# An attention + routed experts + FFN kernel on one Trainium2 core: eight instead of twelve weight-conversion units left to the FFN, rows scaled behind another block, a PSUM bank for the small slot's transposes

## The chip, the cores and the metric

The kernel runs on one core of one Trainium2 chip. The metric is device microseconds (us) of one execution, the median of several runs; lower is better. The engines are named as the profile names them: PE (TensorE, matmuls; PEld is its loading of weights), DVE (VectorE), ACT (ScalarE), POOL (GpSimd) and SP (SyncE, which issues most of the DMAs; SPq is its queue).

## The reference

Three layers follow each other; everything is float32.

```python
# 1. attention, 4 x 12 heads, sequence 448, head size 64
scores = scale * q @ k.T - log(S);  attn = sigmoid(scores);  x = attn @ v
x = x.transpose(0, 2, 1, 3).reshape(1792, 768)
# 2. experts: each row goes to one of 8 experts
expert_idx = argmax(normalised(x) @ normalised(expert_emb).T / tau);  gate_w = its softmax probability
h = maximum(x[mask] @ w1[e], 0)            # w1[e] 768 x 1024
out[mask] = gate_w[mask] * (h @ w2[e])     # w2[e] 1024 x 768
# 3. FFN
h = x @ w_in                               # 768 x 2048
g = h - tanh(h)
return g @ w_out                           # 2048 x 768
```

## The kernel before

A float32 product is made of three matmuls on operands that are split into a rounded high part and the rest (the low part): high by high, high by low, low by high. Splitting an operand costs a cast on ACT (high) and a subtraction on DVE (low). Three stretches follow each other: attention (to about 225 us), the experts (225 to 538 us) and the FFN in two halves of the rows (half 0 to about 793 us, half 1 to 1041 us), then the last scatter of output rows.

**Experts.** The rows that were routed to an expert are gathered into groups. Two groups with rows of the first three batches, `s0` and `s1`, come first, then six slots of up to 256 rows; a further "small slot" of at most 128 rows (`few`) runs behind slot 0. A group is one pass of `group`. It has four blocks `c` of w1: `product` makes two times 18 matmuls into the PSUM tile `pth`, ACT writes the relu `hh` (L925) and DVE its low part `hl` (L926). Then come three blocks of w2, two times 24 matmuls each, into `pty`. `split` (L896 to L899) makes each product's weights ready: ACT casts the raw weights to `ring`, DVE subtracts; `ring` holds four products. So PE waits for ACT's and DVE's splits, and a w2 block also for `hl`.

The next group's rows (`prep`, called by `nxt()` between the w1 and the w2 blocks) are gathered by a DMA that POOL issues (L800), scaled by their gate on ACT (`gate_rows`, L809; in slot 1 on POOL, L818), transposed on PE into `xt` (L840), and split again (ACT L846, DVE L847) into `wi0` and `xl`. When ACT may scale them is set by `issue_after`: for the second group behind the third block's relu, otherwise by `last_few` or by the scheduler.

In the small slot the operands' parts are exchanged: `product` of `few` has the rows as the loaded operand and the weights as the moving one, so that its result has to be turned: `keep` stores it on ACT, `turn` transposes it back on PE into a tile of the `xt` buffers, and `hidden` or `out` read that. `both(c, h)` splits half h of the c-th weight block for it.

**Conversion units.** The FFN's weights come as float64 words. A unit (`conv_steps`) turns one block of 128 columns of w_in or 128 rows of w_out into high and low float32 parts: SP loads `cr` (L1164), ACT takes the absolute value of the high words (L1169), DVE runs four instructions over `ca` (L1171, L1173, L1175, L1177), ACT casts (L1180), DVE subtracts (L1182), SP stores to DRAM (`dwi`, `dwo`, L1184). There are 32 units, in the order wi0, wo0, wi1, wo1 and so on. One runs early in attention; `CPG` says how many run in each group of the experts as long as more than `NFFN` are left; the rest run in FFN half 0, up to `CPF` for each chunk. The experts have three `cr` buffers; the FFN has one, so that its units run one after the other.

**FFN.** In half 0, `act` loads the blocks `wi` and `wo` of f = 0 to 15 from DRAM (L1266, L1269), makes z = y @ w_in (36 matmuls for each f, 18 over 512 and 18 over 384 columns, L1277) and g - tanh on ACT and DVE into `gh` and `gl`; `outp` takes a chunk of two f and adds g @ w_out to the accumulators: 84 matmuls of 384 columns (L1328), seven additions on DVE (L1341). `split(1)` then makes half 1's operands. Half 1 loads the same blocks again.

The order of instructions on each engine is set when the program is built, by the library's scheduler, which works with priorities (`high_priority`) and `issue_after`; each engine then runs its list in order.

```python
                with tc.issue_after(self.xg_act.ins):
                    for _ in range(conv.pop(0)):
                        if len(self.units) > NFFN:
                            with tc.high_priority(offset=LATER):
                                self.conv_unit(*self.units.pop(0), after=self.last_w)
```

In the FFN the same call of `conv_unit` stands in the loop over chunks, behind `act`.

Of the kernel before, what the change touches and what calls it, by code (L numbers as in the profile page):

```python
# [21 lines left out]
LAG = 4  # L22
ROW = 2
ROUTE, ROUTE_E = 8, 3
NEARLY, NFFN = 1, 12
CONV = 14
CPG, CPF = (2, 3, 0, 3, 3, 3, 3, 2), 2
IDLE = 9
LATER = -600
EARLY = -100  # L30
# [2 lines left out]
P = 128  # L33
# [8 lines left out]
class Prog:  # L42
# [721 lines left out]

    def experts_early(self, cx):

        self.last_few = None
        self.pp = self.pool("plan", 1, cx)
        self.mrec = self.pool("mrec", 2, cx)
        self.mx = self.pool("mx", 1, cx)  # L770
        self.mrow = self.pool("mrow", 1, cx)
        wr = self.pool("mrawa", 1, cx)
        self.raws = [wr.tile([P, self.NJ, 256], F32, name=f"w1raw{c}") for c in range(NWE)]
# [31 lines left out]
    def gate_rows(self, s, h):  # L805

        DM, x = self.DM, s["x"]
        with self.tc.issue_after(self.last_few) if self.last_few is not None else ExitStack():
            self.xg_act = self.nc.scalar.activation(x[:, h, :DM], x[:, h, :DM], AF.Copy, scale=x[:, h, DM + 1 : DM + 2])  # L809

    def gather_rows(self, pl, slot, pool=False):
# [61 lines left out]
    def experts(self, cx):  # L873
# [14 lines left out]
        self.last_y = None  # L888
        ps = self.pool("mps", 2, cx, space=PSUM)
        hps = self.pool("mph", 2, cx, space=PSUM, side="right")  # L890

        turns = [0]

# [21 lines left out]
        def group(s, e, new, off, have, nxt, conv, mid=None, last=False, inner=None):  # L915
            hh = hp.tile([P, KF, GR], F32R, tag="hh", name="hh")
            hl = hp.tile([P, KF, GR], F32R, tag="hl", name="hl")
            for c in range(NC1):
                if c >= have:
                    self.weight(e, new, c)  # L920
                pt = hps.tile([P, 2, GR], F32, tag="h", name="pth")
                for u in range(2):
                    product(pt, self.raws[c], s["xt"], NJ, u)
                fs = slice(2 * c, 2 * c + 2)
                relus.append(nc.scalar.activation(hh[:, fs], pt, AF.Relu))  # L925
                nc.vector.scalar_tensor_tensor(hl[:, fs], pt, 0.0, f32(hh[:, fs]), ALU.max, ALU.subtract)  # L926
                if c == 0 and mid is not None:
                    mid()
            self.keep_numbers(s)
            if inner is not None:  # L930
                for c in range(NC2):
                    self.weight(e, new, NC1 + c)
            if nxt is not None:
                nxt()
            if conv:
                with tc.issue_after(self.xg_act.ins):
# [4 lines that stand above are left out]
            for c in range(NC2):  # L941
                if inner is None:
                    self.weight(e, new, NC1 + c)
                if last and c == NC2 - 1:
                    pt = self.last_y = self.lp.tile([P, 2, GR], F32, name="pty_last")
                else:
                    pt = ps.tile([P, 2, GR], F32, tag="y", name="pty")
                for u in range(2):
                    product(pt, self.raws[NC1 + c], (hh, hl), KF, u)
                if pt is not self.last_y:  # L950
                    nc.scalar.copy(self.yT[c][:, :, off], pt)
                if c == 1 and inner is not None:
                    inner()
                if last and c == NC2 - 2:
                    with tc.issue_after(self.last_mm.ins):
                        tc.mark_branch_hint_location("more", "LikelyTaken", engines=[mybir.EngineType.PE])
# [68 lines left out]
        def few(s, nxt):  # L1025
# [18 lines left out]
                return self.yT[k % 3][:, :, NT + P : NT + 2 * P]  # L1044

            def turn(k):
                pt = pst()
                for u in range(2):
                    T(nc.tensor.transpose, pt[:, u, :P], stage(k)[:, u], self.ident)
                return pt[:, :, :P]  # L1050
# [10 lines left out]
            def out(c):  # L1061
                A(nc.scalar.copy, self.yT[c][:, :, ds(oa, P)], turn(NC1 + c))
# [19 lines left out]
            for c in range(NC2):  # L1082
# [6 lines left out]
                    nxt()  # L1089
                else:  # L1090
                    out(c - 1)
                product(NC1 + c, pt, (hh, hl), 1)
                keep(NC1 + c, pt, nc.scalar.copy)
                if c == 0:
                    both(NC1 + 2, 0)
                    both(NC1 + 2, 1)
            T.last = None
            out(NC2 - 1)
            self.last_few = A.last
            turns[0] += 2 * (NC1 + NC2 - 1)  # L1100

        def run(slots, s, conv, first):
# [22 lines left out]
            pl.update(self.plan())  # L1125

        def second():
            with tc.issue_after(relus[-2].ins):
                for h in range(2):
                    self.gate_rows(self.s1, h)  # L1130
            self.columns(self.s1, pst)

        conv = list(CPG)
# [4 lines left out]
        run(list(range(NST)), s, conv, False)  # L1138
        first = lambda: nc.sync.dma_start(f32(self.wi0).rearrange("p a b -> p (a b)"), self.win_s[0].rearrange("p a b -> p (a b)"))
        first()  # L1140
        self.last_few = None
        if NG > NST:
            tot = nc.values_load(self.tot_i[0:1, 0:1], min_val=1, max_val=NG)
            with tc.If(tot > NST, label="more"):
# [319 lines left out]
```

## Time and profile before

| | |
|---|---|
| median of 3 runs | 1051.7 us (1049.59 to 1053.12) |
| profiled execution | 1050.43 us, span in the trace 1048.7 us |
| mean granted TensorE clock | 0.984 |
| PE busy | 992.3 us (95%) |
| DVE busy | 769.3 us (73%) |
| ACT busy | 587.4 us (56%) |
| POOL busy | 222.2 us (21%) |

The profiled execution took 1.7 us more than its span. PE is busy nearly all of the time, so what is to be looked for is the few places where it is not, or where its clock is lowered (a clock of 1.00 is 2.4 GHz, 0.5 is 1.2 GHz). A mean over the span doesn't show those; they are read stretch by stretch.

### The profile page before, as it was taken

What the parts mean: (1) busy time and instruction counts of PE and PEld (TensorE: products, weight loads), DVE (VectorE), ACT (ScalarE), POOL (GpSimd) and SP (SyncE); (2) the same over time, 40 slices, a digit from 0 to 9 for tenths busy, and PEclk for the clock granted to TensorE, in tenths of its full rate; (3) what the DMA queues carried; (4) which work ended last, traced back from release to release, by engine and by line L of the source; (5) the groups of instructions that cost most, each with busy time, mean ns of one, the idle gap of its engine ahead of it and who ended that gap; (6) DMA issues with size and microseconds to landing.
All of it is one profiled execution on the core that took longest, in us unless ns stands there. A gap on an engine that the chain in (4) does not pass through costs nothing.

```text
span 1048.7 us, 16583 instructions
## 1 busy us (share of the span) xinstructions
PE 992.3 (95%) x6318; PEld 921.7 (88%) x6318; DVE 769.3 (73%) x1011; ACT 587.4 (56%) x728; POOL 222.2 (21%) x315
## 2 busy tenths in 40 slices
PE   7999999999999899999999999999819999999997
PEld 5877877789999799999998999988819999999997
DVE  7687777769795699788638887788638766666773
ACT  7788888875575776666536643453217533433340
POOL 8567667554403110300000000000000300000002
PEclk9999999999999999999999999999959999999999
DMA  6433333479459859658326454434355522332312
GB/s 173 138 108 109 103 92 103 154 230 365 169 184 301 271 182 336 218 177 285 128 101 237 134 190 158 180 143 188 113 188 211 194 81 103 121 121 94 117 61 106
DMA packets 83446, 174.87 MB, mean 167 GB/s; under 512 B 7624, under 2 KB 62943, under 8 KB 83359
## 3 DMA queue, kind: packets, MB, share of 16 engines
q1 hardware_dynamic: 79438, 155.56, 43.4%
q0 software_dynamic: 3760, 17.95, 4.9%
q8 instruction: 52, 0.85, 0.3%
q14 instruction: 36, 0.29, 0.1%
q10 hardware_dynamic: 160, 0.21, 0.1%
HBM read 156.28 MB, written 36.30 MB: 184 GB/s over the span
## 4 chain that ended last, share of the span: by engine, by line
issue 57%; PE 6%; POOL 2%; DMA 1%; DVE 0%; ACT 0%; POOLq 0%; ACTq 0%; DVEq 0%
PE pth L908 3%; PE pty L908 2%; POOL out_dram L546 2%; DMA xg<-x_tok,gidx 1%; PE pty L1007 0%; ACT xg L809 0%; PE xt L840 0%; POOLq L1459 0%; DVE ring L899 0%; DVE ca L1175 0%; PE xt L1007 0%; ACT ca L1169 0%; DVE ca L1171 0%; DVE hl L926 0%; DVE xl L847 0%
## 5 line engine op out<-in xcount | busy, mean ns | idle before, releaser
L1328 PE MATMUL o<-wo,gh 128*128 128x384 f32 x896 | 239.7, 336 | 16.9 <-DMA wo<-dwo 12.2
L1277 PE MATMUL z<-yh,wi 128*128 128x512 f32 (+1 forms) x768 | 219.6, 367 | 13.8 <-DMA wi<-dwi 13.4
L1328 PEld LDWEIGHTS o<-wo,gh 128*128 128x128 f32 x896 | 163.3, 188 | 19.6 <-issue 12.5
L1277 PEld LDWEIGHTS z<-yh,wi 128*128 128x128 f32 x768 | 142.3, 189 | 30.5 <-DMA wi<-dwi 13.9
L1328 PE MATMUL o<-wo,gl 128*128 128x384 f32 x448 | 150.4, 336 | 0.0
L908 PE MATMUL pth<-wi,ring 128*128 128x256 f32 x768 | 141.7, 284 | 4.7 <-DVE hl L926 4.0
L546 POOL DMA_INDIRECT out_dram<-acc,toki x14 | 17.4, 1240 | 597.5 <-DVE acc L1341 596.3
L1277 PE MATMUL z<-yl,wi 128*128 128x384 f32 (+1 forms) x384 | 138.9, 366 | 0.0
L908 PE MATMUL pty<-hh,ring 128*128 128x256 f32 x736 | 136.2, 283 | 0.0
L908 PEld LDWEIGHTS pth<-wi,ring 128*128 128x128 f32 x768 | 119.8, 190 | 5.8 <-issue 3.7
L277 DVE TENSOR_TENSOR al<-pq,ah 128x896 fp32r<-128x896 f32 x84 | 91.2, 1087 | 42.8 <-ACT pq L276 42.4
L1341 DVE TENSOR_TENSOR acc<-o,acc 128x768 f32<-128x768 f32 x97 | 92.3, 951 | 38.1 <-PE o L1328 37.8
L908 PEld LDWEIGHTS pty<-hh,ring 128*128 128x128 f32 x736 | 115.7, 191 | 0.1
L908 PE MATMUL pth<-xl,ring 128*128 128x256 f32 x384 | 108.3, 282 | 0.0
L275 ACT ACTIVATE ah<-pq,bias_s 128x896 fp32r<-128x896 f32 x84 | 85.4, 1017 | 34.8 <-PE pq L268 34.1
L908 PE MATMUL pty<-hl,ring 128*128 128x256 f32 x368 | 103.9, 284 | 0.0
L1328 PEld LDWEIGHTS o<-wo,gl 128*128 128x128 f32 x448 | 84.4, 188 | 1.0
L276 ACT ACTIVATE pq<-pq,bias_s 128x896 f32<-128x896 f32 x84 | 83.0, 988 | 0.0
L1277 PEld LDWEIGHTS z<-yl,wi 128*128 128x128 f32 x384 | 72.4, 189 | 7.9
L899 DVE TENSOR_TENSOR ring<-w1raw,ring 128x768 fp32r<-128x768 f32 x64 | 60.5, 952 | 21.4 <-ACT ring L898 21.1
L908 PEld LDWEIGHTS pth<-xl,ring 128*128 128x128 f32 x384 | 73.2, 191 | 0.0
L1298 ACT ACTIVATE s<-t,sq_thr 128x896 f32<-128x896 f32 x32 | 33.5, 1046 | 70.2 <-DVE r L1295 70.2
(319 smaller groups left out, 1903.9 us busy)
## 6 DMA issues: line engine op xcount, KB each, us to landing
w1raw<-in_moe_w_dram SPq DMA_DIRECT2D x36, 768.0 KB
w2raw<-in_moe_w_dram SPq DMA_DIRECT2D x27, 1024.0 KB
wi<-dwi SPq DMA_DIRECT2D x32, 768.0 KB
wo<-dwo SPq DMA_DIRECT2D x32, 768.0 KB
cr<-in_moe_w_in_dram SPq DMA_DIRECT2D x16, 768.0 KB
dwi<-cr SPq DMA_DIRECT2D x16, 768.0 KB
cr<-in_moe_w_out_dram SPq DMA_DIRECT2D x16, 768.0 KB
dwo<-cr SPq DMA_DIRECT2D x16, 768.0 KB
```

What stands on the lines that cost most here:

```text
L275: nc.scalar.activation(hi, pv, AF.Sigmoid, **sc)
L276: self.last_sig = nc.scalar.activation(pv, pv, AF.Sigmoid, **sc)
L277: nc.vector.tensor_tensor(lo, pv, f32(hi), ALU.subtract)
L546: i = self.nc.gpsimd.indirect_dma_start(**kw)
L899: self.last_split = nc.vector.tensor_tensor(wl, cols, f32(wh), ALU.subtract)
L908: self.last_mm = nc.tensor.matmul(pt[:, u], a[:, kk], b[:, kk], start=(n == 0), stop=(n == 3 * K - 1))
L1277: nc.tensor.matmul(z[:, G0[g] : G0[g] + GS[g]], wi[:, a, j * P : (j + 1) * P], yhl[half][g][b][:, j], start=(left[g] == 3 * NJ), stop=(lef ...
L1298: nc.scalar.activation(s2, t, AF.Relu, bias=bias[2])
L1328: nc.tensor.matmul(o[:, w, :NW], a[:, u, i * P : (i + 1) * P], wo[:, b, w * NW : (w + 1) * NW], start=(n == 0), stop=(n == 3 * CH - 1),)
L1341: nc.vector.tensor_tensor(acc[i], ov, acc[i], ALU.add)
```

## The change

Four edits. First, the numbers of conversion units: the FFN keeps 8 instead of 12, and the experts take 23 instead of 19, with one more in the groups `s0`, slot 2, slot 3 and slot 4. Second, ACT may scale the next group's rows only behind the relu of the third of the four w1 blocks, now for every group. Third, `turn` of the small slot takes its PSUM tile from a pool of its own (`mpt`, one buffer) instead of the `xt` buffers. Fourth, in the small slot the second half of the last w2 block is split in the middle of the following block.

```diff
-NEARLY, NFFN = 1, 12
+NEARLY, NFFN = 1, 8
 CONV = 14
-CPG, CPF = (2, 3, 0, 3, 3, 3, 3, 2), 2
+CPG, CPF = (3, 3, 0, 3, 4, 4, 4, 2), 2
...
     def gate_rows(self, s, h):
 
         DM, x = self.DM, s["x"]
-        with self.tc.issue_after(self.last_few) if self.last_few is not None else ExitStack():
+        with self.tc.issue_after(self.rows_after) if self.rows_after is not None else ExitStack():
...
         hps = self.pool("mph", 2, cx, space=PSUM, side="right")
+        tps = self.pool("mpt", 1, cx, space=PSUM)
...
             if nxt is not None:
+                self.rows_after = relus[-2].ins
                 nxt()
...
             def turn(k):
-                pt = pst()
+                pt = tps.tile([P, 2, GR], F32, tag="t", name="tt")
...
                     nxt()
                 else:
                     out(c - 1)
+                if c == 1:
+                    both(NC1 + 2, 1)
                 product(NC1 + c, pt, (hh, hl), 1)
                 keep(NC1 + c, pt, nc.scalar.copy)
                 if c == 0:
                     both(NC1 + 2, 0)
-                    both(NC1 + 2, 1)
             T.last = None
             out(NC2 - 1)
-            self.last_few = A.last
...
         def second():
-            with tc.issue_after(relus[-2].ins):
-                for h in range(2):
-                    self.gate_rows(self.s1, h)
+            self.rows_after = relus[-2].ins
+            for h in range(2):
+                self.gate_rows(self.s1, h)
```

The lines of the changed kernel are numbered one or two higher than before (L908 becomes L909, L1007 L1009, L1184 L1186, L1266 L1268). A number behind a name (`dwi_116`) tells one buffer from another: of `dwi` and `dwo`, block f of w_in is `dwi_` and 88 + 2f, block f of w_out `dwo_` and 89 + 2f, so that `dwi_118` and `dwo_119` are those of f = 15.

Three places show how instructions move. The first is SP's queue at the end of FFN half 0. `cr` loads and `dwi` or `dwo` stores are conversion units; `wi` and `wo` are the FFN's loads. Before:

```order
L1164 DMA cr<-in_moe_w_in_dram 128x6x256
L1184 DMA dwi_116<-cr 128x1536
L1266 DMA wi_124<-dwi_116 128x1536
L1164 DMA cr<-in_moe_w_out_dram 128x1536
L1266 DMA wi_124<-dwi_88 128x1536
L1184 DMA dwo_117<-cr 128x1536
L1269 DMA wo<-dwo_117 128x1536
L1164 DMA cr<-in_moe_w_in_dram 128x6x256
L1184 DMA dwi_118<-cr 128x1536
L1266 DMA wi_9954<-dwi_118 128x1536
```

And now:

```order
L1166 DMA cr<-in_moe_w_in_dram 128x6x256
L1268 DMA wi_10002<-dwi_114 128x1536
L1268 DMA wi_124<-dwi_116 128x1536
L1186 DMA dwi_118<-cr 128x1536
L1166 DMA cr<-in_moe_w_out_dram 128x1536
L1271 DMA wo<-dwo_113 128x1536
L1271 DMA wo<-dwo_115 128x1536
L1268 DMA wi_10002<-dwi_118 128x1536
L1186 DMA dwo_119<-cr 128x1536
L1268 DMA wi_124<-dwi_88 128x1536
```

Before, each load of a `wi` or `wo` stood right behind the store that it reads; now the last stores stand ahead of loads of earlier blocks, `dwo_119` ahead of half 1's first load (`dwi_88`).

The second place is ACT's list from the end of the small slot into the w1 blocks of slot 1. `ring` casts are splits of slot 1's weights, `xg` is the next slot's rows, `ca<-cr` a conversion unit. Before:

```order
L1007 COPY yT_last<-xt 128x2x128
L809 ACTIVATE xg<-xg 128x768 x4
L1169 ACTIVATE ca<-cr 128x768
L898 CAST ring<-w1raw_142 128x768
L1169 ACTIVATE ca<-cr 128x768
L925 ACTIVATE hh<-pth 128x512
L898 CAST ring<-w1raw_2714 128x768 x2
L925 ACTIVATE hh<-pth 128x512
```

And now:

```order
L1009 COPY yT_last<-tt 128x2x128
L899 CAST ring<-w1raw_142 128x768
L926 ACTIVATE hh<-pth 128x512
L899 CAST ring<-w1raw_2714 128x768 x2
L926 ACTIVATE hh<-pth 128x512
L899 CAST ring<-w2raw_2715 128x1024 x2
L926 ACTIVATE hh<-pth 128x512
L809 ACTIVATE xg<-xg 128x768 x2
L1171 ACTIVATE ca<-cr 128x768 x2
L899 CAST ring<-w2raw_2716 128x1024 x2
L926 ACTIVATE hh<-pth 128x512
```

The rows' scaling and the conversion units went from ahead of the slot's second w1 block to behind its third relu (the fourth relu and two splits are now behind them).

The third place is the end of DVE's list for the experts, in the last slot (the names are those of `split`, `hl` and the conversion units; the `TENSOR_LOAD` is the experts' last row). Before:

```order
L926 SCALAR_TENSOR_TENSOR hl<-pth,hh 128x512
L899 TENSOR_TENSOR ring<-w1raw_2714,ring 128x768 x2
L926 SCALAR_TENSOR_TENSOR hl<-pth,hh 128x512
L899 TENSOR_TENSOR ring<-w2raw_2715,ring 128x1024 x2
L926 SCALAR_TENSOR_TENSOR hl<-pth,hh 128x512
L899 TENSOR_TENSOR ring<-w2raw_2716,ring 128x1024 x2
L926 SCALAR_TENSOR_TENSOR hl<-pth,hh 128x512
L899 TENSOR_TENSOR ring<-w2raw_2717,ring 128x1024 x2
L1143 TENSOR_LOAD tot_i
```

And now:

```order
L900 TENSOR_TENSOR ring<-w2raw_2716,ring 128x1024
L927 SCALAR_TENSOR_TENSOR hl<-pth,hh 128x512
L1179 SCALAR_TENSOR_TENSOR ca<-cr,ca 128x768
L1173 TENSOR_SCALAR ca<-ca 128x768
L1175 TENSOR_SCALAR ca<-ca 128x768
L900 TENSOR_TENSOR ring<-w2raw_2717,ring 128x1024
L1177 SCALAR_TENSOR_TENSOR ca<-cr,ca 128x768
L1184 TENSOR_TENSOR cr<-ca,cr 128x768
L1179 SCALAR_TENSOR_TENSOR ca<-cr,ca 128x768
L900 TENSOR_TENSOR ring<-w2raw_2717,ring 128x1024
L1184 TENSOR_TENSOR cr<-ca,cr 128x768
L1145 TENSOR_LOAD tot_i
```

Before, no conversion instruction stood in this stretch; now seven stand among the last splits. From the last-but-one slot's fourth `hl` to the end of the experts it is 30 instructions of conversion units on DVE, where it was 10.

## Rows read from the trace of the kernel before

**Rows 1.** The page's busy line: busy us (share of the span) xinstructions

```profile
PE 992.3 (95%) x6318; PEld 921.7 (88%) x6318; DVE 769.3 (73%) x1011; ACT 587.4 (56%) x728; POOL 222.2 (21%) x315
```

**Rows 2.** Waits of PE: who waits <- what ended it: us, times, longest

```profile
PE z L1277 <- DMA wi<-dwi: 13.4, 1, 13.4
PE o L1328 <- DMA wo<-dwo: 12.2, 1, 12.2
PE o L1328 <- DVE acc L1341: 4.7, 5, 1.9
PE pth L908 <- DVE hl L926: 4.0, 3, 3.0
PE xt L1007 <- DVE row L852: 1.2, 1, 1.2
```

**Rows 3.** PE's timeline, 748 to 790 us: start, duration, instructions [idle before, its releaser]

```profile
748.81 0.62 PE L1277 MATMUL z<-yh,wi 128*128 128x512 f32 x2
...
753.03 0.51 PE L1277 MATMUL z<-yh,wi 128*128 128x384 f32 x2
...
768.56 0.98 PE L1328 MATMUL o<-wo,gh 128*128 128x384 f32 x2 [12.25 <-DMA wo<-dwo]
...
784.19 1.22 PE L1277 MATMUL z<-yh,wi 128*128 128x512 f32 x2 [13.37 <-DMA wi<-dwi]
...
789.90 0.51 PE L1277 MATMUL z<-yh,wi 128*128 128x384 f32 x2
```

**Rows 4.** Timeline of SP's queue in FFN half 0

```profile
572.76 0.32 SPq L1184 DMA_DIRECT2D dwi<-cr  x1
...
721.34 0.32 SPq L1184 DMA_DIRECT2D dwo<-cr  x1
...
756.77 0.37 SPq L1184 DMA_DIRECT2D dwo<-cr  x1
...
776.58 0.32 SPq L1184 DMA_DIRECT2D dwi<-cr  x1
```

**Rows 5.** Windows: stretch us, PE, PEld, DVE, ACT, POOL busy (xinstructions), clock, DMA share, GB/s

```profile
367.00:377.00 10.00, 9.88 (x70) 9.91 (x71) 10.00 (x14) 6.63 (x9) 0.00 (x0) 0.83 0.29 107
450.00:486.00 36.00, 36.00 (x306) 35.94 (x306) 30.00 (x38) 22.75 (x31) 0.00 (x0) 1.00 0.65 222
486.00:521.00 35.00, 35.00 (x297) 34.94 (x296) 26.49 (x33) 20.47 (x28) 0.00 (x0) 1.00 0.46 153
521.00:538.00 17.00, 17.00 (x144) 17.00 (x142) 6.84 (x9) 6.57 (x8) 0.00 (x0) 1.00 0.16 52
756.00:785.00 29.00, 3.38 (x10) 2.50 (x9) 10.44 (x12) 7.28 (x8) 0.00 (x0) 0.57 0.55 189
```

**Rows 6.** Groups of DVE instructions, 225 to 538 us: xcount, busy us, mean ns, idle before

```profile
L1182 DVE TENSOR_TENSOR cr<-ca,cr 128x768 fp32r<-128x768 f32 x19 | 18.0, 948 | 0.7 <-ACT cr L1180 0.5
L1171 DVE TENSOR_SCALAR ca<-ca 128x768 f32<-128x768 f32 x19 | 10.4, 550 | 7.4 <-ACT ca L1169 7.4
```

**Rows 7.** ACT's timeline, where it scales rows around slot 1 and later

```profile
358.77 3.42 ACT L809 ACTIVATE xg<-xg 128x768 f32<-128x768 f32 x4
...
434.38 0.94 ACT L809 ACTIVATE xg<-xg 128x768 f32<-128x768 f32 x1 [4.00 <-DMA xg<-x_tok,gidx]
```

**Rows 8.** Timeline of POOL and PE at the small slot, and of a later gather

```profile
325.64 4.51 POOL L818 TENSOR_SCALAR xg<-xg 128x768 f32<-128x768 f32 x2 [2.98 <-DMA xg<-x_tok,gidx]
...
334.76 0.38 PE L1007 MATMUL xt<-ident,yT 128*128 128x128 f32 x2
...
342.96 0.60 PE L840 MATMUL xt<-ident,xg 128*128 128x128 f32 x4
...
419.77 9.16 POOL L800 DMA_INDIRECT xg<-x_tok,gidx  x1 [0.30 <-DVE ca L1175]
```

**Rows 9.** Waits of SP's queue, 225 to 538 us

```profile
SPq L868 <- DVE ring L899: 118.2, 40, 8.0
...
SPq L1184 <- DVE cr L1182: 28.2, 17, 4.2
```

More of the change, by code (lines that the diff above doesn't have):

```diff
@@ L765, in experts_early @@
     def experts_early(self, cx):
-        self.last_few = None
+        self.rows_after = None
         self.pp = self.pool("plan", 1, cx)
@@ L1140, in experts @@
         first()
-        self.last_few = None
+        self.rows_after = None
         if NG > NST:
```

## The prediction

> **What bounds the kernel now.** I read the busy line first: PE works 992.3 of 1048.7 us [rows 1]. The other engines have room on the mean, so a change that leaves PE's 6,318 matmuls alone can gain only where PE stands still or runs at the lower clock. The table of PE's waits says where. Two single waits of 13.4 and 12.2 us are in the FFN, for loads of `wi` and `wo`; behind them stand five waits for the additions (4.7), three for `hl` in the experts (4.0) and one for `row` in the small slot (1.2) [rows 2].
>
> PE's timeline puts the two large ones side by side [rows 3]. z of f14 ends at 768.56 − 12.25 = 756.31. PE then waits for wo14, does six o, which take from 768.56 to 784.19 − 13.37 = 770.82, and waits for wi15. The six o take 2.26 us; 384 columns at the full clock cost (756.31 − 753.03)/18 = 0.182 us, so 1.2 us are lost. The 18 wide z that follow take 5.71 us, where the block before took 4.22: 1.5 lost. That stretch shows a granted clock of 0.57 [rows 5], near the lower level, 1.2 GHz, behind two idle times. In sum 12.25 + 13.37 + 1.2 + 1.5 = 28.3 us.
>
> SP's queue says why. The stores of the FFN's conversion units come one cycle of some 21 us apart (572.76 for the first, 721.34 for the eighth: 148.6/7), because one `cr` buffer is filled, converted and stored before it is filled again [rows 4]. The eleventh unit, wi15, is stored at 776.58, PE starts on it at 784.19; wo14 is stored at 756.77 and used at 768.56, 11.8 us later. The chain of twelve is longer than the half's matmuls. Neither ACT nor DVE is short there (7.28 and 10.44 busy of 29 us) [rows 5].
>
> **The change part by part.** *Eight units in the FFN.* The chain then ends with its eighth store, at 721 by the present cycle, and wo15 is usable 11.8 us later, at 733; wi15, one cycle before, at 712. When does PE ask for it? In the changed program's order, counted, 541 z and 492 o stand ahead of f15's first z. At 748.81 PE had done 504 z and 588 o. So it asks at 748.8 + 37 × 0.208 − 96 × 0.182 = 739 us (0.208 is 7.5 us for 36 z [rows 3]). wi15 is there 27 us ahead, wo15 6 us even if it were asked for at once. Nothing is left of the stall: **−28.3**. The bound on the other side is a chain that is later by half a cycle and more, where half of it stays: −14.
>
> The four moved units cost DVE work elsewhere: a unit is three instructions of 0.948 and two of 0.550 us, 3.94 us [rows 6]. In slots 2 to 4 DVE is busy 30.0 of 36 us [rows 5], so one unit fits in the 6.0 that are idle. Its load and its store, 0.79 MB each, are 44 GB/s more in those 36 us, on 222 GB/s at a DMA share of 0.65 [rows 5]: about 0.78, no term. It is tighter at the end: from the last-but-one slot's fourth `hl` to the experts' end 30 conversion instructions stand, where 10 stood. Of the 20 more, 13 come in the first 35 us, 13 × 0.79 = 10.3 us where 35.0 − 26.49 = 8.5 are idle, and 7 in the last 17 us, 5.5 where 10.2 are idle [rows 5]. 1.8 us are over. Bounds: nothing, if they slide into the last stretch, and 1.8 with a lower clock behind it (1.7, next part), 3.5. I take **+1.5**, near the row's 1.8, as nothing forbids sliding.
>
> In the FFN four units less free DVE of 15.8 us, and the additions on which PE waits come earlier: of 4.7 us [rows 2] between 0 and 4.7; I take half, **−2.5**, since the order of z and o changes as well.
>
> *Rows scaled behind the third relu.* In slot 1 four scalings of rows, 3.42 us, stand on ACT ahead of the second block's `ring` casts [rows 7]. DVE's `hl` comes late, PE waits 3.0 us at 364 [rows 2], and the stretch behind it has 70 matmuls in 10.0 us where slot 3 has 306 in 36.0, or 85: 15 too few, 1.76 us, of which 0.12 is idle, at a clock of 0.83 [rows 5]. Later one scaling waits 4.00 us for its gather, with the block's casts queued behind it [rows 7]; it is one of the two other waits for `hl`, together 1.0 [rows 2]. Behind the third relu the gather has landed and the first splits are through. 3.0 + 1.6 + 0.7 of that 1.0: **−5.3**; bounds −3.0, if the clock falls for another reason, and −5.6.
>
> What is late next? Two scalings (1.7) and two conversions' first steps (1.7) now stand ahead of the fourth relu and of two `ring` casts. The ring holds four products, about 2 × 2.1 + 2 × 2.85 us of PE's work, so a delay of 3.4 us is covered unless DVE is behind too. That cover is gone where DVE is full; then each of five groups loses up to 1.3 us, 6.5. I take **+1**.
>
> *The bank of its own.* `turn` no longer shares buffers with the next slot's rows, and PE's wait for `row`, 1.2 us [rows 2], can go; bounds 0 and −1.2; **−0.7**. But slot 1's rows are now asked for sooner: their transposes stood at 342.96, and their new place is right behind the 27th matmul of the small slot, where the first `turn` is now, at 334.8 [rows 8]. POOL scaled them at 325.64 + 4.51 = 330.15 after a wait of 2.98 for the gather [rows 8]; behind the later gather that this gives, some 4.2 us (the 37 w2 matmuls that now stand ahead of the small slot's own transposes, at 36.0/306 = 0.118 [rows 5]), they end at 334.4. The margin shrinks from 12.8 to 0.4 us. I take **+1**; bounds 0 and 8, the 8.2 us that the transposes moved forward.
>
> *The half split in another place*: 0 here; it is one cast and one subtraction, and two blocks of matmuls lie ahead of their use. *The half's turn*: `dwo_119` is now ahead of half 1's first load in SP's queue, but stored by 721; the operands of half 1 come straight behind a stretch without pauses: **+0.5**, bounds 0 and 2.
>
> Sum: −28.3 − 5.3 − 0.7 − 2.5 + 1.5 + 1 + 1 + 0.5 = −32.8. Against the profiled execution that is 1050.4 − 32.8 = 1017.6; against the median, which is 1.3 higher, 1019. I say **1018**. All terms at their better ends give 1050.4 − 28.3 − 5.6 − 1.2 − 4.7 = 1010.6; at the worse ones 1050.4 − 14 − 3 + 3.5 + 6.5 + 8 + 2 = 1053, which needs five causes at once; the single causes are the cases below.
>
> **A rule against the change.** A gather issued by POOL at 419.77 took 9.16 us and was released by L1175, a conversion's instruction on DVE with two inputs [rows 8]. The Trainium skill, page "SBUF — State Buffer", section "SBUF: two separate sides", says that a DVE instruction in a two-port mode, or one with two SBUF inputs against a POOL instruction that reads SBUF, shuts POOL out for its whole length, and that in a two-port mode POOL can't write a DMA's descriptors. The trace agrees in that one place. By that rule the 20 more DVE instructions would hold gathers up; without it the sum stays as it stands. What it would do here is the third rival.
>
> **The rivals.**
> 1. *The stall is only moved.* The chain ends 10 to 14 us later than 733, and PE waits for wo15 or the half's start. For it: the units now alternate with other loads in SP's queue, with stores ahead of loads. Against: 6 to 27 us of margin. Half of 28.3 comes back: 1018 + 14 = about 1033.
> 2. *DVE becomes the bound in the experts.* For it: 30.0 of 36 busy [rows 5], one more unit makes 33.9. If `hl` is late by 3.0 with 1.6 of clock in five groups: 23, so 1041. Against: 2 us stay idle.
> 3. *POOL is held up.* If slot 1's rows come late by a whole gather of 9.16 us [rows 8] (an upper end, as its usual length would come off), PE waits 9.2 − 0.4 = 8.8 and loses 1.6 of clock: 1018 + 10 = 1028. Against: POOL's list is the same as before, and the slow gather stood far from the small slot, at 419.77.
> 4. *Slower: stores hold up weight loads.* SP waits in its list for DVE's last conversion instruction, 28.2 us over 17 stores, 4.2 at the most, and weight loads wait up to 8.0 us for the splits [rows 9]. If with four more units raw weights come a full 8.0 late in five groups (the four with more units and the last), that costs 5 × (8.0 + 1.6) = 48: 1066. It decides from 32.8/5 = 6.6 us for a group. Against: PE waits for no raw weight at all [rows 2].
> 5. *No gain.* PE waits at the half's turn instead, as ACT and DVE had used the 28 us to catch up: 1045 to 1050. Against: they are idle for most of them [rows 5].
>
> **How the numbers follow.** The forecast, with its own range 1011 to 1024, has 0.66; the stall moved 0.07; DVE full 0.10; POOL held up 0.08; slower 0.05; no gain 0.04. 1011 to 1034 holds the forecast, the first and the third rival, 0.81. A measurement here tells a difference from about 0.3%, 3.2 us (the three runs lie 3.5 apart). Forecast, rivals 1 to 3 and a quarter of the fifth are faster: 0.92; same 0.03; slower 0.05.
>
> **What would show it.** In PE's waits the two lines for DMA wi and wo are gone and no wait over 2 us stands between 720 and 790; the eighth store is near 715 to 720; the chunk with f15 runs at a clock of 1.00. In slot 1 no wait for `hl` over 1 us, and some 85 matmuls in the 10 us that had 70. Mean clock about 0.99 and over. Wrong would be: a new wait of z or o for a DMA late in half 0 (rival 1), waits for `hl` or `ring` in slots 2 to 5 (2), a wait of `xt` for `xg` near 335 (3), waits of pth or pty for raw weights, or of ACT's casts for them (4), or an idle time at half 1's first z (5).

## The result and the profile after

| | before | changed |
|---|---|---|
| median | 1050.64 us (4 runs, 1048.44 to 1053.12) | 1014.26 us (4 runs, 1012.8 to 1015.34) |
| ratio | | 0.9652, 95% interval 0.9626 to 0.9679 |
| span of the profiled execution | 1048.7 us | 1011.1 us |
| mean granted clock | 0.984 | 0.999 |

The change is faster by 36 us; 33 were forecast, to 1018, in a range of 1011 to 1034. The busy line of the changed kernel's page, to be read against [rows 1]:

```profile
PE 986.3 (98%) x6318; PEld 918.9 (91%) x6318; DVE 766.3 (76%) x1011; ACT 586.1 (58%) x728; POOL 225.0 (22%) x315
```

The same 6,318 matmuls are 98% of a span that is 37.6 us shorter. The waits of PE in the changed kernel, against [rows 2] (who waits <- what ended it: us, times, longest):

```profile
PE pth L909 <- ACT ring L899: 1.5, 2, 0.7
...
PE z L1279 <- ACT yh L1254: 1.1, 1, 1.1
...
PE o L1330 <- DVE acc L1343: 0.7, 1, 0.7
...
PE pth L909 <- DVE hl L927: 0.6, 1, 0.6
```

The two lines for `wi` and `wo` are gone, the additions cost 0.7 instead of 4.7, `hl` 0.6 instead of 4.0. New are the two waits for `ring` casts on ACT, the one for `yh` (at the same place PE waited 0.4 us before) and, in lines that are left out here, two of 0.4 us in the small slot. PE's first z says where the gain was made (timeline of PE, before and then after; start, duration, instructions, idle before):

```profile
538.62 0.70 PE L1277 MATMUL z<-yh,wi 128*128 128x512 f32 x2 [0.41 <-PEq L1144]
```

```profile
534.31 0.97 PE L1279 MATMUL z<-yh,wi 128*128 128x512 f32 x3 [1.06 <-ACT yh L1254]
...
1003.56 0.34 PE L1330 MATMUL o<-wo,gh 128*128 128x384 f32 x1
```

The FFN starts 4.3 us sooner. From there to the end of its last o at 1003.9 it takes 469.6 us; before, the last o ended at 1041.5, 502.9 us behind its first z. So 33.3 us come from the FFN and 4.3 from what lies ahead of it. Not all of these 4.3 are the experts': their first matmul, too, comes 0.9 us sooner (PE, before and then after):

```profile
223.16 0.37 PE L908 MATMUL pth<-wi,ring 128*128 128x256 f32 x1
```

```profile
222.30 0.37 PE L909 MATMUL pth<-wi,ring 128*128 128x256 f32 x1
```

From that matmul to the first z the experts take 315.46 us before and 312.01 now, 3.45 less. In the fourteen kernels of this document their first matmul starts between 222.25 and 224.30 us, and in two whose programs are alike up to the FFN (before and e3_two_cr) it lies 0.4 us apart; so experts are compared below from their first matmul on. SP's queue of the changed kernel has the chain's first and eighth store, against [rows 4]:

```profile
568.44 0.32 SPq L1186 DMA_DIRECT2D dwi<-cr  x1
...
718.80 0.32 SPq L1186 DMA_DIRECT2D dwo<-cr  x1
```

A cycle is (718.80 − 568.44)/7 = 21.5 us, as long as before; there are only fewer. The windows of the changed kernel (columns as in [rows 5]) are slot 1, slot 3, the last two slots and the end of FFN half 0:

```profile
360.00:370.50 10.50, 10.50 (x92) 10.50 (x91) 6.00 (x8) 7.36 (x10) 0.00 (x0) 1.00 0.24 76
444.51:480.50 35.99, 35.99 (x306) 35.93 (x306) 32.76 (x42) 25.12 (x34) 0.00 (x0) 1.00 0.68 236
480.50:516.00 35.50, 35.50 (x302) 35.44 (x302) 33.98 (x45) 25.23 (x35) 0.00 (x0) 1.00 0.78 273
516.00:533.00 17.00, 17.00 (x144) 17.00 (x143) 12.24 (x15) 7.16 (x9) 0.00 (x0) 1.00 0.49 190
720.00:760.00 40.00, 40.00 (x219) 38.31 (x218) 30.41 (x31) 19.55 (x22) 0.00 (x0) 1.00 0.28 103
```

Slot 1 runs at the full clock, with 92 matmuls in 10.5 us where there were 70 in 10.0. DVE is fuller in the slots (32.8 to 34.0 of some 36 us) and PE still doesn't wait in these windows. At the end of FFN half 0 PE is busy all of the time.

### The profile page after: what moved, and what is told of

The parts are those of the page before. It is cut to its first block, busy times and chain, and to the rows that moved or that the text cites. A ratio compares the mean times of both kernels' runs of the same rounds, so it can differ in the third digit from the quotient of the medians.

```text
span 1011.1 us, 16597 instructions
## 1 busy us (share of the span) xinstructions
PE 986.3 (98%) x6318; PEld 918.9 (91%) x6318; DVE 766.3 (76%) x1011; ACT 586.1 (58%) x728; POOL 225.0 (22%) x315
## 4 chain that ended last, share of the span: by engine, by line
issue 57%; PE 27%; ACT 5%; DVE 3%; DMA 3%; POOL 3%; SPq 1%; POOLq 0%; ACTq 0%; DVEq 0%
PE pth L909 7%; PE pty L909 6%; PE pav L291 6%; PE pq L268 4%; POOL out_dram L546 2%; ACT ah L275 1%; ACT pq L276 1%; PE pr L316 1%; DMA xg<-x_tok,gidx 1%; DVE al L277 1%; SPq L199 1%; DMA kq<-in_q_dram 1%; ACT sq L333 1%; PE pth L1009 1%; PE xt L840 1%
## 5 line engine op out<-in xcount | busy, mean ns | idle before, releaser
L909 PE MATMUL pth<-wi,ring 128*128 128x256 f32 x768 | 139.3, 282 | 2.7 <-ACT ring L899 1.5
L909 PE MATMUL pty<-hh,ring 128*128 128x256 f32 x736 | 138.6, 285 | 0.0
L909 PEld LDWEIGHTS pth<-wi,ring 128*128 128x128 f32 x768 | 118.1, 188 | 3.5 <-ACT ring L899 1.9
L909 PEld LDWEIGHTS pty<-hh,ring 128*128 128x128 f32 x736 | 115.8, 191 | 0.6 <-DVE ring L900 0.5
L909 PE MATMUL pth<-xl,ring 128*128 128x256 f32 x384 | 107.5, 280 | 0.0
L909 PE MATMUL pty<-hl,ring 128*128 128x256 f32 x368 | 103.8, 283 | 0.0
L899 ACT CAST ring<-w1raw 128x768 fp32r<-128x768 f32 x64 | 52.8, 835 | 46.8 <-PE pty L909 24.5
L1295 DVE TENSOR_TENSOR r<-z,t 128x896 f32<-128x896 f32 x32 | 34.9, 1090 | 55.4 <-ACT th L1289 55.0
```

The source lines that it names most:

```text
L899: self.last_high = nc.scalar.copy(wh, cols)
L909: self.last_mm = nc.tensor.matmul(pt[:, u], a[:, kk], b[:, kk], start=(n == 0), stop=(n == 3 * K - 1))
```

## The experiments

All ratios are against the kernel before, run beside each. The theory at the start: nearly all of the gain is the FFN's shorter chain of units; the rows' edit takes the waits for `hl` away; the bank and the half split are small. The rivals were those of the prediction. The last column is the time from the experts' first matmul to the first z in the profiled execution (before 315.5, changed 312.0).

| run | what | median us | ratio (95% interval) | first z us | experts us |
|---|---|---|---|---|---|
| e1_units_only | only the numbers of units | 1019.24 | 0.9703 (0.968 to 0.9727) | 540.00 | 316.5 |
| e2_rest_only | only the other three edits | 1052.33 | 1.0024 (1.0005 to 1.0042) | 537.99 | 315.7 |
| e3_two_cr | before, half units, two half buffers in the FFN | 1033.9 | 0.9848 (0.9824 to 0.9872) | 538.54 | 315.8 |
| f1_no_rows | changed, without the rows' edit | 1020.24 | 0.97 (0.9675 to 0.9726) | 541.36 | 318.2 |
| f2_no_bank | changed, without the bank | 1015.43 | 0.9658 (0.9632 to 0.9683) | 535.42 | 313.0 |
| f3_no_split | changed, without the split's move | 1013.62 | 0.9643 (0.9617 to 0.9669) | 534.37 | 311.8 |
| e7_ten | changed, 10 units in the FFN | 1026.46 | 0.9769 (0.9745 to 0.9793) | 545.58 | 322.5 |
| g3_ten_early | the same, other slots | 1017.75 | 0.9684 (0.965 to 0.9718) | 533.70 | 310.2 |
| g5_22 | changed, 9 units in the FFN | 1013.77 | 0.965 (0.9624 to 0.9676) | 534.33 | 311.6 |
| g2_23_early | changed, 8 units, other slots | 1012.75 | 0.9637 (0.9612 to 0.9663) | 536.53 | 312.2 |
| g4_25 | changed, 6 units in the FFN | 1033.87 | 0.9853 (0.9815 to 0.9891) | 542.57 | 319.3 |
| e8_four | changed, 4 units in the FFN | 1048.44 | 0.9972 (0.9954 to 0.999) | 541.88 | 318.6 |

### The units alone, and the rest alone

```diff
 e1_units_only, against before
-NEARLY, NFFN = 1, 12
+NEARLY, NFFN = 1, 8
-CPG, CPF = (2, 3, 0, 3, 3, 3, 3, 2), 2
+CPG, CPF = (3, 3, 0, 3, 4, 4, 4, 2), 2
```

> Only the numbers of conversion units are changed (8 in the FFN, 23 in the experts); rows, bank and half split as before. Theory (the stall at the end of FFN half 0 is the length of the chain of units): both waits for wi and wo go, with the low clock behind them, 28.3 us, and most of the 4.7 us of waits for the additions; slot 1's wait of 3.0 us with its clock stays. 1050.6 - 28.3 - 4 = 1018, between 1015 and 1022. Rival (more units in the experts need the other edits, since ACT and DVE run the splits late otherwise): new waits for hl or ring in the slots with four units, 2 us and more each with the clock behind them, 1024 or above.

Measured 1019.24: the theory. From first z to last o the FFN takes 1011.0 − 540.0 = 471.0 us. The experts are 1.1 us longer than before; PE's waits for `hl` in them are still there (from the same view):

```profile
PE pth L908 <- DVE hl L926: 3.6, 3, 1.9
...
PE pth L908 <- DVE ring L899: 1.1, 2, 0.6
```

The rest alone is the changed kernel with that diff taken back:

```diff
 e2_rest_only, against the changed kernel
-NEARLY, NFFN = 1, 8
+NEARLY, NFFN = 1, 12
-CPG, CPF = (3, 3, 0, 3, 4, 4, 4, 2), 2
+CPG, CPF = (2, 3, 0, 3, 3, 3, 3, 2), 2
```

> The other three edits without the numbers of units (12 in the FFN, 19 in the experts). Theory: the experts gain what the trace of the changed kernel showed there, 4 to 5.5 us, and the two waits for wi and wo stay as long as they were, because the chain of units starts with the FFN: about 1046, between 1044 and 1048. Rival: the chain doesn't start sooner by what the experts gain, and the stall takes it back: 1049 to 1051.

Measured 1052.33, 0.24% above before, less than the 0.3% from which a measurement here tells a difference: neither. The expected 1046 was wrong, and so was the reason of the rival. PE's waits in this kernel:

```profile
PE z L1279 <- DMA wi<-dwi: 13.6, 1, 13.6
PE o L1330 <- DMA wo<-dwo: 12.3, 1, 12.3
PE o L1330 <- DVE acc L1343: 3.9, 4, 2.0
PE pth L909 <- ACT ring L899: 2.9, 4, 0.7
PE xt L840 <- POOL xg L818: 0.8, 1, 0.8
PE pty L909 <- ACT ring L899: 0.7, 1, 0.7
```

The stall is what it was, so it moves with the FFN's start. But the experts gain nothing: their first z comes 0.6 us sooner and their first matmul 0.9. With the waits for `hl` gone (0.7 left), five waits of 0.73 us for `ring` come in, one a slot, and one for POOL's scaling. The changed kernel has two of those five; its own rows show how such a wait arises (ACT, then PE, in slot 1):

```profile
375.29 0.84 ACT L1182 CAST cr<-ca 128x768 fp32r<-128x768 f32 x1 [0.94 <-DVE ca L1179]
376.06 0.83 ACT L899 CAST ring<-w1raw 128x768 fp32r<-128x768 f32 x1
```

```profile
376.95 0.39 PE L909 MATMUL pth<-wi,ring 128*128 128x256 f32 x1 [0.73 <-ACT ring L899]
```

A conversion's cast on ACT waits for DVE's step before it; the next slot's first `ring` cast stands behind it, and PE, which has one matmul of the next slot early in its list, waits for that cast.

### Which of the three edits counts beside the units

The three kernels take one edit back each, in the changed kernel:

```diff
 f1_no_rows, against the changed kernel
             if nxt is not None:
-                self.rows_after = relus[-2].ins
                 nxt()
...
             out(NC2 - 1)
+            self.last_few = A.last
...
 f2_no_bank, against the changed kernel
-                pt = tps.tile([P, 2, GR], F32, tag="t", name="tt")
+                pt = pst()
...
 f3_no_split, against the changed kernel
-                if c == 1:
-                    both(NC1 + 2, 1)
...
                 if c == 0:
                     both(NC1 + 2, 0)
+                    both(NC1 + 2, 1)
```

> The changed kernel with the rows scaled as before (behind the small slot's last work for all groups behind it, not behind the third relu); units, bank and half split as changed. Theory (the edit of the rows takes the waits for hl in slot 1 and later away): PE again waits for hl in slots 1 and 3, some 2 and 1.5 us as with the units alone, with a lower clock behind them: about 1018.5, 4 us and more above the changed kernel. Rival (the gain in the experts comes from the bank, or from a new order of the lists): within 2 us of the changed kernel, 1013 to 1016.

> The changed kernel with the small slot's transposes in the buffers of xt again, as before. Theory: PE's wait for row (1.17 us) and the one of 0.29 us beside it come back and slot 1's rows are transposed some 8 us later, with no further loss: 1015.5, between 1014 and 1017. Rival (the earlier rows of slot 1 carry the gain of the other edits, since ACT and DVE are freer there): 1018 and above.

> The changed kernel with both halves of the small slot's last w2 block split at the end of its first w2 block, as before. Theory: nothing hangs on it, within 1.5 us of the changed kernel, 1013 to 1016; at most the two waits of 0.4 us in the small slot move. Rival (the cast and the subtraction stand ahead of the small slot's hidden parts and delay them): a wait for hl of 1 us and more in the small slot with a lower clock behind it, 1017 and above.

Without the rows' edit 1020.24, and experts that take 6.2 us longer; the edit is worth some 6 us here (f3_no_split, run beside it, has 1013.62). Not all of that is `hl`, whose wait is back in slot 1 (1.88 us) and not in slot 3. The larger part is PE's wait for POOL in the small slot (POOL's timeline of f1_no_rows, then PE's):

```profile
322.06 6.82 POOL L800 DMA_INDIRECT xg<-x_tok,gidx  x1 [0.30 <-issue]
...
336.23 2.20 POOL L818 TENSOR_SCALAR xg<-xg 128x768 f32<-128x768 f32 x1 [5.08 <-DMA xg<-x_tok,gidx]
```

```profile
338.48 1.54 PE L840 MATMUL xt<-ident,xg 128*128 128x128 f32 x6 [3.27 <-POOL xg L818]
...
340.10 4.12 PE L1008 MATMUL pth<-ring,wi 128*128 128x256 f32 x18
```

Here the second gather takes 6.82 us, its rows come late, and PE waits 3.27 us for the scaling; behind the wait the granted clock is 0.66 (335 to 342 us), and the next 18 matmuls take 4.12 us. In the changed kernel the same two places read:

```profile
325.27 2.82 POOL L800 DMA_INDIRECT xg<-x_tok,gidx  x1 [0.30 <-issue]
...
334.42 2.21 POOL L818 TENSOR_SCALAR xg<-xg 128x768 f32<-128x768 f32 x1 [1.12 <-DMA xg<-x_tok,gidx]
```

```profile
336.95 0.82 PE L840 MATMUL xt<-ident,xg 128*128 128x128 f32 x6
...
337.74 2.40 PE L1009 MATMUL pth<-ring,wi 128*128 128x256 f32 x18
```

Scaled at 336.63, transposed from 336.95: 0.3 us to spare. The 18 matmuls that took 4.12 us take 2.40 here, at a clock of 1.00. Counted from the experts' first matmul, f1_no_rows is 5.7 us behind the changed kernel at the small slot's last matmul, 8.9 behind at slot 1's last w1 block, with the wait for `hl`, and 6.2 at the first z, as the changed kernel's two waits for `ring` casts aren't there.

Without the bank, 1015.43: the wait of 1.17 for `row` and the one of 0.28 are back, and the experts take 1.0 us longer; the theory's size, though the intervals of the two kernels overlap. The split's move does nothing (1013.62). So four kernels with 8 units (the split apart) show how rows and bank depend on each other. Neither (e1_units_only): the experts take 316.5 us. Rows alone (f2_no_bank): 313.0. The bank alone (f1_no_rows): 318.2. Both: 312.0. The rows' edit is worth 3.5 us without the bank and 6.2 with it; the bank without the rows costs 1.7, because it brings slot 1's transposes forward to rows that are not there yet. These are single traces; by the medians it is 3.8 and 6.0 for the rows, and 1.0 for the bank, which is within noise.

Why that gather is long, before and e1_units_only say, which differ in the numbers of units alone. The second gather of slot 1 before, then in e1_units_only with DVE's last instruction ahead of its end:

```profile
320.86 1.80 POOL L800 DMA_INDIRECT xg<-x_tok,gidx  x1 [0.30 <-issue]
```

```profile
322.42 6.83 POOL L800 DMA_INDIRECT xg<-x_tok,gidx  x1 [0.30 <-issue]
...
327.48 0.94 DVE L1007 TENSOR_TENSOR ring<-w1raw,ring 128x768 fp32r<-128x768 f32 x1
```

With one unit more in the group `s0`, DVE has no pause from 316 to 328.42 us there, where it stood idle for 1.6 us before; the gather ends at 329.25, 0.83 us behind DVE's last instruction. That is so everywhere: in the fourteen traces each of the 35 gathers of the experts that took over 2.5 us ends 0.82 to 0.83 us behind the end of a DVE instruction of a split or of a unit.

### How the chain of units is made up

```diff
 e3_two_cr, against before
-            self.conv_pools(cx, 1)
+            self.conv_pools(cx, 2)
+            self.cvw = DM // 2
+            self.units = [(src[:, k * src.shape[1] // 2 : (k + 1) * src.shape[1] // 2], dst[:, :, k * DM // 2 : (k + 1) * DM // 2])
+                          for src, dst in self.units for k in range(2)]
...
-            for _ in range(CPF if c else 0):
+            for _ in range(2 * CPF if c else 0):
...
-        W = self.DM
+        W = self.cvw
```

> The kernel before, with 12 units in the FFN as before, but each cut into two half units of 64 rows or columns' words, with two half-size cr buffers instead of one. Same bytes, same work but for twice as many, half as long instructions. Theory (a unit waits for the one before to be stored, as there is one buffer): two are under way at a time, the chain of 12 ends before 735, both waits go: 1016 to 1026. Rival (the chain is as long as it is because its steps wait in ACT's and DVE's lists behind other work): the last store is later than 770, and 15 us and more of the stall stay: 1036 or above.

Measured 1033.9, between the two; by its own test, the last store, the rival is the nearer. The wait for `wo` is gone and 4.7 us are left for `wi`, in two waits. The FFN takes 486.0 us, 16.9 less than before. Its order of z and o is that of before (594 o ahead of f15's first z, where the changed kernel has 468), so a shorter chain gains without another order. First and last store in SP's queue:

```profile
573.86 0.65 SPq L1184 DMA_DIRECT2D dwi<-cr  x1
...
771.71 0.52 SPq L1184 DMA_DIRECT2D dwo<-cr  x1
```

With two buffers the chain is 198 us instead of 219. The waits of SP's queue in the FFN's first half say on what it still waits:

```profile
SPq L1184 <- DVE cr L1182: 87.0, 14, 10.9
...
SPq L1164 <- DMA dwi<-cr: 17.9, 10, 5.4
SPq L1164 <- DMA dwo<-cr: 15.1, 9, 4.7
```

In the chain SP waits 87.0 us for the units' last step on DVE, and 33.0 us for stores to land. One unit of before, at the place of the stall, shows it row by row (SP's queue, ACT and DVE):

```profile
724.98 0.43 SPq L1164 DMA_DIRECT2D cr<-in_moe_w_in_dram  x1
731.52 0.91 ACT L1169 ACTIVATE ca<-cr 128x768 f32<-128x768 f32 x1
...
739.54 0.96 DVE L1182 TENSOR_TENSOR cr<-ca,cr 128x768 fp32r<-128x768 f32 x1
740.53 0.32 SPq L1184 DMA_DIRECT2D dwi<-cr  x1
744.23 0.66 SPq L1164 DMA_DIRECT2D cr<-in_moe_w_out_dram  x1
```

From load to first step 6.5 us, from there to the store 9.0, of which ACT and DVE work on it 5.7, and 3.7 until the next load. So steps that wait in ACT's and DVE's lists behind the FFN's own work are a part of the cycle, and the one buffer is not all of it. Two buffers of full size were not run, so how the cycle divides is not shown.

### How many units the FFN and the experts stand

The text of the second expectation below gives the spread of its kernel in a wrong way, and that of the first has s0 and s1, not s0 and slot 0, with three; the diffs have the numbers. The eight numbers are s0, s1 and slots 0 to 5.

```diff
 against the changed kernel's NFFN = 8 and CPG (3, 3, 0, 3, 4, 4, 4, 2)
+NFFN = 10, CPG (3, 3, 0, 3, 3, 3, 4, 2)    e7_ten
+NFFN = 10, CPG (3, 3, 0, 4, 4, 3, 2, 2)    g3_ten_early
+NFFN = 9,  CPG (3, 3, 0, 3, 4, 4, 3, 2)    g5_22
+NFFN = 8,  CPG (4, 4, 0, 4, 3, 3, 3, 2)    g2_23_early
+NFFN = 6,  CPG (3, 3, 0, 4, 5, 4, 4, 2)    g4_25
+NFFN = 4,  CPG (3, 3, 0, 4, 5, 5, 5, 2)    e8_four
```

> The changed kernel with 10 units in the FFN and 21 in the experts (s0, slots 0, 2, 3 three each, slot 4 four). Theory (the chain's length against PE's demand): two units more are two cycles of some 18 to 20 us, so the last two stores stand near 737 and 756 and are usable 12 us later, at 749 and 768; PE asks for wi15 near 744 and for wo15 near 763. Two waits of about 5 us come back, with a lower clock behind them: 1020 to 1027. Rival (there is a margin of tens of us, any number up to ten does as well as eight): 1013 to 1016.

> The changed kernel with 6 units in the FFN and 25 in the experts (slot 1 as before, slot 2 four, slot 3 and 4 four, one of them five: s0 3, s1 3, slots 1 to 5: 3, 4, 5, 4, 4 with the last slot's two, in the order of the list). Theory (units that the experts don't finish slide to the FFN's start, where yh takes the place of their buffers in SBUF, and PE waits until the last one is stored): with 23 units the last store stands at 528.0 and PE waits 1.06 us, with 27 the last two stand at 560.5 and 565.5 and PE waits 23 us; two units fewer than those 27 come one or two cycles of 8 to 15 us earlier, and PE waits 5 to 15 us with a low clock behind it: 1020 to 1033. Rival (the loss with 27 came from DVE being full in the slots): waits for hl or ring inside slots 3 to 5, and less than 3 us at the FFN's start.

*Ten.* 1026.46 is in the theory's range for another reason. (The profiled execution took 1029.44 us, the longest of the four.) No wait for a DMA is in its FFN; 475.0 us from first z to last o are 5.4 more than in the changed kernel, 3.7 of it waits for additions and their issue around 745. The program's order had put f15's z later (540 z and 564 o ahead of it), which my sum for this kernel had left out. The rest is in the experts, which take 322.5 us, 10.5 more than in the changed kernel. ACT in the last slot of e7_ten:

```profile
522.43 0.89 ACT L1171 ACTIVATE ca<-cr 128x768 f32<-128x768 f32 x1 [6.00 <-DMA cr<-in_moe_w_out_dram]
523.22 1.03 ACT L899 CAST ring<-w2raw 128x1024 fp32r<-128x1024 f32 x1
524.15 0.59 ACT L926 ACTIVATE hh<-pth 128x512 fp32r<-128x512 f32 x1
```

```profile
524.80 0.38 PE L909 MATMUL pty<-hh,ring 128*128 128x256 f32 x1 [2.36 <-ACT hh L926]
```

ACT waits 6.00 us for a conversion's load, with a split and a relu behind it, and PE stands 2.36 us, then 0.55 and 0.50. In the 31 us from 515 it does 189 matmuls at a granted clock of 0.89, where the changed kernel's 31 us up to the same place (503.7 to 534.7) have 251 at a clock of 1.00. That is the way in which the fourth rival was to make the kernel slower, with the unit's load in place of the weights'.

> The changed kernel with 10 units in the FFN and 21 in the experts, spread as s0 and s1 three each, slot 1 and 2 four, slot 3 three, slots 4 and 5 two each (in the other kernel with 10 units slot 4 had four and the ones before three). Theory (the 11 us that that kernel lost in the experts came from one load of cr that ACT waits 6.0 us for, with the last slot's casts behind it, and not from the number of units): no such wait with two units asked for in slot 4; the experts end as in the changed kernel or 1 us earlier, and the FFN keeps its waits of 4 to 5 us for additions: 1016 to 1021. Rival (a wait of that kind comes with any 10 units, or the FFN's loss is larger): 1024 and above.

Measured 1017.75, as the theory has it: the number of units is the same, no such wait stands in the last slots, and the experts take 310.2 us, 12.3 less than in e7_ten. The FFN keeps its wait of 3.6 us for an addition, and takes 476.6 us.

*More than 23 in the experts.*

> The changed kernel with only 4 units in the FFN and 27 in the experts (slot 1 four, slots 2 to 4 five each). Theory (DVE is nearly full in the experts at four units for a slot, 32.8 to 34.0 of 36 us busy): a fifth unit's 3.9 us don't fit; slots 2 to 4 lose 1 to 2 us each and the last slots some 4 with the clock behind it, while the FFN gains nothing more, as it has no wait left: 1020 to 1030. Rival (the conversions have the lowest priority and slide into later gaps): 1013 to 1017.

1048.44 was far outside. PE's waits in e8_four, and DVE and ACT at the FFN's start:

```profile
PE z L1279 <- DVE yh L1254: 14.5, 1, 14.5
PE z L1279 <- ACT yh L1254: 8.9, 1, 8.9
PE z L1279 <- DMA wi<-dwi: 5.8, 2, 3.0
```

```profile
564.50 0.96 DVE L1184 TENSOR_TENSOR cr<-ca,cr 128x768 fp32r<-128x768 f32 x1 [0.94 <-ACT cr L1182]
568.85 1.03 DVE L1254 CAST yh<-yT 128x768 fp32r<-128x768 f32 x2 [3.39 <-DMA dwo<-cr]
```

The slots themselves lose nothing: 430 to 470 us has PE busy for 40.0 of 40.0 with DVE at 35.1. What the experts don't finish slides to their end. The first of the two large waits (8.9) is for an ACT cast of `yh` that stands behind conversions in its list and then, by its releaser, waits for one of DVE's conversion steps. The second (14.5) is for the other tile of `yh`, which is not written until the last `cr` store has landed: by that releaser it stands where the experts' buffers stood. With 25 units (1033.87, 0.9 us above the theory's range) the waits are 9.5 and 0.7 for `yh` and 5.4 for `wi`. The changed kernel has the first sign of it; DVE, whose second line is what ACT's cast and then PE's 1.06 us above wait for:

```profile
527.01 0.95 DVE L1184 TENSOR_TENSOR cr<-ca,cr 128x768 fp32r<-128x768 f32 x1
532.56 1.03 DVE L1254 CAST yh<-yT 128x768 fp32r<-128x768 f32 x2 [4.60 <-DMA dwo<-cr]
```

> The changed kernel with 9 units in the FFN and 22 in the experts (slot 4 three instead of four). Theory: the last unit in the experts is stored 8 us and more before the FFN, so that the wait for yh of 1.06 us goes; the FFN's chain is one cycle of 19 us longer and still early enough, with 1 to 3 us of waits for additions: 1013 to 1017, the same as the changed kernel. Rival (what the FFN waits for is the last store even so): one wait for wi or wo of 3 us and more near its half's end, 1018 and above.

> The changed kernel with the same 23 units in the experts, spread otherwise: s0 and s1 four each, slot 1 four, slots 2 to 4 three each, the last two. Theory (what counts for the FFN's start is when the last store stands; with fewer units queued late it stands some us earlier): the wait of 1.06 us for yh goes, and one of the two waits of 0.73 us: 1012 to 1014. Rival (three cr buffers let only so many units through before the end, wherever they are asked for): last store at 528 or later, 1014 to 1016; or the units asked for early push ACT's casts back, 1017 and above.

With 22 units the last store stands at 524.98, the wait for `yh` is gone, and the time is the same, 1013.77: the theory. With 23 units asked for earlier 1012.75 is in the theory's range, but its mechanism did not come: the last store still stands at 530.23 and the wait for `yh` is still 1.0 us, as the rival said (the profiled execution took 1015.58 us, 2.8 above the median). Whether the three `cr` buffers or the lists hold the units back was not tried. It is the lowest median, but its runs overlap with those of the changed kernel and of g5_22; no run here beats the changed kernel beyond noise.

## Why the prediction was right, step by step

- **The stall.** Forecast −28.3 and gone, as the main part of the FFN's 33.3; e1_units_only gives nearly the same FFN without the other edits (471.0 us for 469.6). The chain was as forecast: eighth store at 718.8 (721 forecast), wi15 loaded from 710.6 on, no wait. When PE asks was forecast too late: not at 739 but at 726.1, for one z of f15 that stands alone, and at 730.5 for the others (these have the counted 541 z and 492 o ahead of them). The FFN began 4.3 us sooner and the additions, too, waited less. So from the load's issue to PE's asking there were 15.5 us; the wide margin that the prediction had put at 27 us covered the error. That one buffer makes the cycle was only partly right: two half buffers in e3_two_cr took 21 us off a chain of 219. That doesn't touch the sum, which took the cycle's length from rows.
- **The additions.** Mis-sized: −2.5 forecast, 0.7 − 4.7 = −4.0 measured. With the stall's 28.3 that makes 32.3 of the FFN's 33.3.
- **The rows' scaling.** −5.3 and +1 for what is late next. `hl` costs 0.6 instead of 4.0, and slot 1 has its clock. What came next was not the fourth relu but `ring` casts behind conversions: 1.5 us in the changed kernel, 3.6 with 12 units. The step that was wrong is that the edit is worth something by itself: e2_rest_only shows that it isn't, in that order of the lists. Beside the units it is worth 3.5 us, and 6.2 with the bank, most of them at the small slot's rows, which the prediction had not counted for it. All of the experts' terms together were forecast at −2.5 (−5.3, +1, −0.7, +1, +1.5) and came to −3.45: near, with terms that partly made up for each other.
- **The bank.** −0.7 forecast; −1.2 between f2_no_bank and the changed kernel, inside their noise, and no gain where the rows' edit is missing. Two waits of 0.4 (for `hl` and `ring` in the small slot) take part of the place of 1.2 and 0.3. The margin for POOL, forecast at 0.4 us and +1, was 0.3, and nothing waited, but that the margins agree is luck. The prediction had slot 1's transposes right behind the 27th matmul, at 334.8, and the rows scaled at 334.4. In the changed kernel two transposes stand there (334.35), six more stand 18 matmuls further back, and the last rows are scaled at 336.63. In f1_no_rows the six stand where the prediction had them, and PE waits for them.
- **DVE in the last slots.** +1.5 forecast. The instructions slid, as the lower bound had it: no wait in the last slots, 0.65 us more at the FFN's start (1.06 for 0.41).
- **The half split and the half's turn.** The first 0, as f3_no_split shows; for the second, +0.5, no wait stands there.

Of the rivals, the third (POOL) showed in the small slot of f1_no_rows, e2_rest_only (0.8) and e7_ten (0.3), not in the changed kernel. By the rule cited with it (the Trainium skill, "SBUF — State Buffer", "SBUF: two separate sides") DVE would be what holds POOL; the trace agrees. With one unit less in `s0` the gather of 6.83 us takes 1.80, and each long gather ends 0.82 to 0.83 us behind a DVE instruction's end. In 30 of the 35 that instruction reads two operands in SBUF (a split's subtraction, or a unit's step over `ca` and `cr`); in 5 it is a unit's step with one. The second rival's price was paid at another place, the FFN's start, with 25 and 27 units. The fourth's mechanism showed in e7_ten. Why the lists fall well for one set of numbers and badly for another was seen in each, not derived: the scheduler's order decides it.

## What to carry to other kernels

Read a stall at the end of a chain back to its cycle, and then ask for each part of the cycle what it waits for: a buffer, or its place in a list. Work that is moved to fill an engine's gaps is not free when the gaps are used up by a late load (ACT waits with everything behind it) or when the next stage needs the memory that it holds; look at the first instruction behind the stage's end, where the changed kernel's 1 us was the first sign of what two units more would cost. Edits in a kernel whose order a scheduler makes should be tried together and apart, as their gains don't add up here: −30 and +2.7 apart, −36 together.

## What the runs showed of the hardware that was not expected

- By its releaser, the next stage's first write of `yh` waits until the last store from `cr` has landed: 4.6 us from issue to that write in the changed kernel. With 27 units the last store is issued at 565.48 and the write starts at 568.85, at the end of PE's wait of 14.5 us.
- A gather that POOL issues took 1.80 us in one kernel, 2.82 and 6.82 in others at the same place of the program, and 9.16 elsewhere [rows 8]. The long ones end 0.82 to 0.83 us behind a DVE instruction's end; where DVE works on without a pause, the gather goes on with it.
- What such a stop costs is more than its waits: in e8_four, with 8.9, 3.0 and 14.5 us of waits, the granted clock is 0.69 over 533 to 583 us, and 74 matmuls are done there.
